# Decode attention with a sliding window: output projection on two column groups, and one more pair of K loads in 32 KB rows

## The chip, the cores and the metric

The kernel runs on one core of a Trainium2 chip. The metric is the device time of one execution in microseconds (us). Each execution also has a span, from its first to its last instruction, some 1.7 us shorter.

## The reference

One query token for each of 32 batch rows, 32 query heads on 8 KV heads, the last 512 positions of a cache of 2048:

```python
q = (x @ wq).reshape(B, Sq, Hq, Dh).transpose(0, 2, 1, 3)      # x 32x512, wq 512x4096
k = repeat(k_cache[:, :, Sk - W:, :], 4); v = repeat(v_cache[:, :, Sk - W:, :], 4)   # W = 512
p = softmax(q @ k.T * Dh ** -0.5)
out = (p @ v).transpose(0, 2, 1, 3).reshape(B, Sq, Hq * Dh) @ wo   # wo 4096x512
```

K and V are 33.5 MB each, wq and wo 4.2 MB each: 75.5 MB to read, very little arithmetic.

## The kernel before

The cache window is cut into 16 K chunks and 16 V chunks of 2 MB (128 rows of 16 KB). K goes through three buffers and V through four. Every load is issued by SyncE (SP), in the order of a list; each other engine has a list of its own. In the lists, `T8.1` is the second of two VectorE transposes of K chunk 8, `S2` the scores of quad 2 on TensorE, `M2` their maximum on VectorE, `E`, `N`, `C` softmax steps on ScalarE, `P2` the turn of the probabilities, `Z1.0` to `Z1.3` the spread of quad 1's probabilities into a masked operand (VectorE and ScalarE share it), `V0` a product P x V.

```python
DMA_ORDER = "K0 B0 K1 V0 K2 K3 K4 K5 V1 K6 K7 K8 V2 K9 K10 K11 V4 K12 K13 K14 V6 K15 V8 ... V15"
V_PAIRED = (2, 4, 6)                      # these V loads carry two chunks, in 32 KB rows
...
# SP: a K load waits until its buffer (of NK = 3) has been transposed
if n >= NK:
    sp.wait_ge(dve_T, 2 * (n - NK + 1))
sp.dma_start(K_sb[:, n % NK]..., cache_rows(k_cache, n)).then_inc(sem_k[n % NK], 16)
...
# TensorE, output projection: four column groups of 128 outputs
for c in range(4):
    pe.matmul(X_ps[32*c:32*(c+1), 2, 0:128], lhsT=o_sel[:, i, hg, :],
              rhs=wo_sb[:, hg, i, c*128:(c+1)*128], ..., tile_position=(0, 32*c))
...
# then two casts on VectorE (c = 0, 1) and two on ScalarE (c = 2, 3), and the output DMA
```

## Time and profile before

| | before |
|---|---|
| time, 3 executions at first | 187.28 us (187.22 to 187.29) |
| time, all 51 executions in this study | 187.22 to 187.77 us |
| loads | 75.5 MB in one queue, 16 DMA engines busy throughout |
| busiest compute engine | VectorE, 71% |

The loads are served by 16 DMA engines, and one packet is one row of a load: the packet records show 128 packets of 16 KB for a load of 2 MB, and 16 in flight at a time. The queue runs dry when fewer are, but for the tens of ns of a handover from packet to packet. A load is "ahead" when its issue comes before the packets in front of it have been worked off. Below, **lead** is the time from the start of a load's issue to its first packet; the prediction subtracts the 0.54 us of the issue itself. (Where the load in front has rows of the same size, as for K13, the first packet is counted off in order of start. On the engine furthest ahead it comes some tenths of a us sooner: in e13 K12's first packet at 100.03 and eight packets of 613 ns give an estimate of 104.9 for K13, the count 105.5.) The profile lines of before, of an execution of 187.45 us, stand in the prediction.

### The profile page before, as it was taken

How to read it: one execution, taken by the hardware profiler on the slowest of the kernel's cores; microseconds unless marked ns; L12 is line 12 of the kernel's file. 1: busy time of each engine (PE TensorE's matmuls, PEld its weight loads, DVE VectorE, ACT ScalarE, POOL GpSimd, SP SyncE). 2: the span in 40 equal slices, each digit the busy share in tenths (PEclk: the TensorE clock that was granted, in tenths of full speed). 3: DMA queues.
4: the chain of work that ended last, by engine and by line, in shares of the span. 5: the costliest groups of instructions: out<-in, count | busy, mean ns of one | idle time of the engine just before them, and what ended most of it. 6: DMA issues, size and time to landing. Idle time of an engine off the chain costs nothing.

```text
span 185.7 us, 3839 instructions
## 1 busy us (share of the span) xinstructions
PE 108.6 (58%) x1604; PEld 88.0 (47%) x1604; DVE 131.4 (71%) x239; ACT 82.6 (44%) x142; POOL 31.2 (17%) x82
## 2 busy tenths in 40 slices
PE   0220303447048983199504996438999995999852
PEld 0100001132038771199203496207987894999741
DVE  0018696999999999939999489999999946510001
ACT  3000100139620069610893033977959899911011
POOL 7100029510600236000330140000021000000000
PEclk9999999999756999759955599655899999699999
DMA  6999999999999999999999999999999999999980
GB/s 201 427 441 420 438 430 416 441 420 438 423 413 441 416 441 445 399 438 420 438 446 402 430 427 427 462 409 406 432 420 434 423 420 434 416 430 407 403 324 24
DMA packets 5872, 75.80 MB, mean 408 GB/s; under 512 B 672, under 2 KB 864, under 8 KB 1888
## 3 DMA queue, kind: packets, MB, share of 16 engines
q1 hardware_dynamic: 5808, 75.53, 96.3%
q8 instruction: 12, 0.20, 0.4%
q10 hardware_dynamic: 48, 0.03, 0.1%
q14 instruction: 4, 0.03, 0.0%
HBM read 75.53 MB, written 0.03 MB: 407 GB/s over the span
## 4 chain that ended last, share of the span: by engine, by line
DMA 45%; PE 22%; DVE 20%; issue 6%; SPq 4%; ACT 0%; DVEq 0%
DMA K_sb<-in_k_cache_dram 26%; PE O_ps L360 14%; DVE KT_sb L436 12%; DMA w_sb<-in_wo_dram 12%; DMA V_sb<-in_v_cache_dram 8%; PE S_ps L321 7%; DVE w_sb L458 6%; SPq L216 2%; DVE maxv L443 2%; PE PT_ps L340 1%; SPq L210 1%; SPq L203 1%; SPq L197 0%; ACT P_bf L506 0%; PE X_ps L397 0%
## 5 line engine op out<-in xcount | busy, mean ns | idle before, releaser
L436 DVE STREAM_TRANSPOSE KT_sb<-K_sb 128x2048 uint32<-128x2048 uint32 x32 | 73.0, 2298 | 13.1 <-DMA K_sb<-in_k_cache_dram 13.0
L360 PE MATMUL O_ps<-w_sb,V_sb 128*128 128x128 bf16 x640 | 42.1, 230 | 3.7 <-DVE w_sb L458 3.1
L360 PEld LDWEIGHTS O_ps<-w_sb,V_sb 128*128 128x128 bf16 x640 | 40.8, 103 | 6.1 <-DVE w_sb L458 3.9
L525 ACT ACTIVATE w_sb<-PTc,mask 128x512 bf16<-128x512 bf16 x60 | 38.5, 730 | 0.0
L270 POOL COPY QBD<-QA_sb 32x64 bf16<-32x64 bf16 x64 | 24.8, 529 | 78.8 <-PE S_ps L321 56.3
L321 PE MATMUL S_ps<-KT_sb,QBD 128*32 128x512 bf16 x256 | 22.3, 504 | 18.1 <-POOL QBD L270 11.0
L458 DVE TENSOR_SCALAR w_sb<-PTc,mask 128x512 bf16<-128x512 bf16 x100 | 30.8, 379 | 0.0
L340 PE MATMUL PT_ps<-P_bf,pick 128*128 128x128 bf16 x128 | 12.6, 277 | 29.8 <-ACT P_bf L506 25.5
L340 PEld LDWEIGHTS PT_ps<-P_bf,pick 128*128 128x128 bf16 x128 | 10.9, 128 | 33.5 <-ACT P_bf L506 28.3
L321 PEld LDWEIGHTS S_ps<-KT_sb,QBD 128*32 128x32 bf16 x256 | 8.3, 115 | 28.7 <-issue 13.8
L497 ACT ACTIVATE X_ps<-S_ps,negmax 128x512 f32<-128x512 f32 x8 | 5.3, 657 | 30.7 <-DVE negmax L445 30.7
L535 ACT ACTIVATE oT_sb<-O_ps 128x128 bf16<-128x128 f32 x8 | 5.9, 741 | 23.9 <-PE O_ps L360 23.9
L525 ACT ACTIVATE K_sb<-PTc,mask 128x512 bf16<-128x512 bf16 x24 | 15.4, 723 | 1.6 <-DVE KT_sb L436 1.6
L360 PE MATMUL O_ps<-K_sb,V_sb 128*128 128x128 bf16 x256 | 15.1, 217 | 1.2 <-DMA V_sb<-in_v_cache_dram 1.2
L360 PEld LDWEIGHTS O_ps<-K_sb,V_sb 128*128 128x128 bf16 x256 | 14.5, 96 | 1.9 <-issue 1.9
L458 DVE TENSOR_SCALAR K_sb<-PTc,mask 128x512 bf16<-128x512 bf16 x40 | 10.7, 347 | 4.4 <-ACT PTc L516 4.4
L360 PE MATMUL O_ps<-KT_sb,V_sb 128*128 128x128 bf16 x128 | 9.1, 240 | 2.5 <-DMA V_sb<-in_v_cache_dram 2.5
L360 PEld LDWEIGHTS O_ps<-KT_sb,V_sb 128*128 128x128 bf16 x128 | 8.9, 108 | 2.6 <-issue 2.6
L301 PE MATMUL X_ps<-w_sb,oT_sb 128*32 128x512 bf16 x32 | 3.8, 626 | 10.6 <-DMA w_sb<-in_wq_dram 10.6
L516 ACT ACTIVATE PTc<-PT_ps 128x512 bf16<-128x512 f32 x8 | 4.8, 594 | 10.5 <-PE PT_ps L340 10.5
L479 DVE CAST K_sb<-S_ps 128x256 bf16<-128x256 f32 x1 | 0.4, 424 | 12.7 <-PE S_ps L372 12.7
L506 ACT ACTIVATE P_bf<-X_ps,recip 128x512 bf16<-128x512 f32 x8 | 5.5, 687 | 8.0 <-DVE recip L451 8.0
(41 smaller groups left out, 49.5 us busy)
## 6 DMA issues: line engine op xcount, KB each, us to landing
K_sb<-in_k_cache_dram SPq DMA_DIRECT2D x16, 2048.0 KB, 17.2
V_sb<-in_v_cache_dram SPq DMA_DIRECT2D x10, 2048.0 KB, 17.0
V_sb<-in_v_cache_dram SPq DMA_DIRECT2D x3, 4096.0 KB, 24.3
w_sb<-in_wq_dram SPq DMA_DIRECT2D x2, 2048.0 KB, 11.8
w_sb<-in_wo_dram SPq DMA_DIRECT2D x7, 512.0 KB, 20.0
w_sb<-in_wo_dram SPq DMA_DIRECT2D x1, 384.0 KB, 21.4
w_sb<-in_wo_dram SPq DMA_DIRECT2D x1, 128.0 KB, 17.5
oT_sb<-in_x_dram ACTq DMA_DIRECT2D x1, 32.0 KB, 4.4
```

The source lines that it names most:

```text
L270: pool.tensor_copy(dst[:, i, :, x0:x0 + 4], src).then_inc(pool_qbd, 1)
L301: ins = pe.matmul(X_ps[32 * c:32 * c + 32, k, :], lhsT=xT_sb[:, kt, :], rhs=w_sb[:, kt, c * 1024 + k * 512:c * 1024 + (k + 1) * 512], star ...
L321: ins = pe.matmul(S_ps[32 * c:32 * c + 32, q % 2, :], lhsT=QBD[:, q % 2, g, b, e, :], rhs=bass.AP(tensor=KT_sb, offset=s0 * slot + (b * G ...
L340: ins = pe.matmul(PT_ps[:, r, :], lhsT=pick[:, r, KS - s:KS - s + P], rhs=P_bf[:, s, :], start=(s == 0), stop=(s == KS - 1), tile_position ...
L360: ins = pe.matmul(O_ps[:, q % 2, 0:P], lhsT=V_sb[:, m % NV, r, :], rhs=z_of(q)[:, :, x0 + r, :], start=(e == 0 and r == 0), stop=(e == 1 a ...
L436: dve.transpose(KT_w[:, n % NK, b].rearrange("p i r s -> p r i s"), K_w[:, n % NK, :, 32 * b:32 * b + 32],).then_inc(dve_T, 1)
L458: ins = dve.tensor_scalar(z_of(q)[:, k].rearrange("p x r -> p (x r)"), PTc[:, q % RING].rearrange("p x r -> p (x r)"), mask[:, k:k + 1], N ...
L497: act.activation(P_f32, S_ps[:, q % 2, :], ACTF.Exp, bias=negmax[:, q:q + 1], scale=SCALE, accum_out=sums[:, q:q + 1],).then_inc(act_exp, 1)
L506: act.activation(P_bf[:, :, :], P_f32.rearrange("p (x s) -> p s x", s=KS), ACTF.Copy, scale=recip[:, q:q + 1],).then_inc(act_P, 1)
L516: act.activation(PTc[:, q % RING], PT_ps[:, :, :].rearrange("p r x -> p x r"), ACTF.Copy).then_inc(act_PT, 1)
L525: ins = act.activation(z_of(q)[:, k].rearrange("p x r -> p (x r)"), PTc[:, q % RING].rearrange("p x r -> p (x r)"), ACTF.Copy, scale=mask[ ...
L535: act.activation(oT_sb[:, :, 4 * q:4 * q + 4].rearrange("p h a -> p a h"), O_ps[:, q % 2, 0:P].rearrange("p (a h) -> p a h", a=4), ACTF.Co ...
```

## The change

The intent is to shave the two ends of a kernel that is bound by its loads: fewer, larger rows in the stream, and a shorter tail of projection and casts after the last load. The order lists were reworked to match the pair.

```diff
-  K0 B0 K1 V0 K2 K3 K4 K5 V1 K6 K7 K8 V2 K9 K10 K11 V4 ...          (DMA_ORDER)
+  K0 B0 K1 K2 V0 K3 K4 K5 K6 V1 K7 K8 V2 K9 K10 V4 ...
-  ... S4 P4 S5 V4 P5 V5 ...                                          (PE_ORDER)
+  ... S4 P4 V4 S5 V5 P5 ...
-  ... T9.0 T9.1 T10.0 Z2.0 T10.1 M4 Z2.1 T11.0 R4 Z2.2 T11.1 Z2.3 M5 R5 T12.0 T12.1 ...   (DVE_ORDER)
+  ... T9.0 T9.1 Z2.0 Z2.1 M4 Z2.2 T10.0 R4 Z2.3 T10.1 T11.0 T11.1 T12.0 M5 T12.1 R5 ...
   (further small moves in DVE_ORDER and ACT_ORDER, and the semaphore counts of the pair, left out)
+  K_PAIRED = (10,)
-  if n >= NK:
-      sp.wait_ge(dve_T, 2 * (n - NK + 1))
+  k = 2 if n in K_PAIRED else 1
+  if n + k > NK:
+      sp.wait_ge(dve_T, 2 * (n - NK + k))
-  K_sb[:, n % NK]..., cache_rows(k_cache, n)
+  K_sb[:, n % NK:n % NK + k]..., cache_rows(k_cache, n, k)
-  for c in range(4):   X_ps[32*c:32*(c+1), 2, 0:128], rhs=wo_sb[:, hg, i, c*128:(c+1)*128]
+  for c in range(2):   X_ps[32*c:32*(c+1), 2, 0:256], rhs=wo_sb[:, hg, i, c*256:(c+1)*256]
-  two casts of 32x128 on VectorE, two on ScalarE
+  one cast of 32x256 on VectorE, one on ScalarE
```

The wait line: for K10 with `k = 2` it is `dve_T >= 18`, both transposes of K8. K10 alone waited for 16, those of K7.

## The prediction

> **What bounds the kernel now.** I read the page first for the shares of the span, then the two DMA rows.
>
> ```profile
> span 185.7 us, 3839 instructions
> PE 108.6 (58%) x1604; PEld 88.0 (47%) x1604; DVE 131.4 (71%) x239; ACT 82.6 (44%) x142; POOL 31.2 (17%) x82
> ...
> DMA  6999999999999999999999999999999999999980
> GB/s 201 427 441 420 438 430 416 441 420 438 423 413 441 416 441 445 399 438 420 438 446 402 430 427 427 462 409 406 432 420 434 423 420 434 416 430 407 403 324 24
> ...
> q1 hardware_dynamic: 5808, 75.53, 96.3%
> q8 instruction: 12, 0.20, 0.4%
> ```
>
> No compute engine is above 71%, but the DMA engines stand at 9 in every slice between the first and the last two, and the load queue q1 alone fills 96.3% of sixteen engines' span. I then went to the packet records in the trace. Between 15 us and 178 us I find no moment at which fewer than 16 packets are in flight, so the queue never runs dry. This is a streaming kernel: a head of 1.8 us before the first packet, a stream, and a tail. Everything inside the stream (transposes, softmax, the spread of P, the PV products) only matters if it starves the queue, that is, if an issue comes later than the end of the packets ahead of it.
>
> The waits of the DMA issuer show that it does wait, but early enough:
>
> ```profile
> SPq L203 <- DVE KT_sb L436: 98.4, 13, 13.0
> SPq L210 <- PE O_ps L360: 38.9, 7, 17.9
> ```
>
> A 98.4 us wait looks like the bound and is not. Setting the issue of each load against its first packet gives the lead: smallest at K chunk 8 (issue done at 59.4, first packet at 61.4, so 2.0 us), 3.0 us at K5, 4.2 us at K7, and 5 to 20 us for the others after the start.
>
> The chain of waits shows the tail:
>
> ```profile
> 161.09 21.45 DMA w_sb<-in_wo_dram
> 182.53 0.04 issue
> 182.58 0.59 PE X_ps L397 x16
> 183.17 0.02 issue
> 183.19 0.28 DVE oT_sb L482
> 183.47 0.31 DVEq L72
> ```
>
> and the timeline the two evacuations behind it:
>
> ```profile
> 183.19 0.57 ACT L552 ACTIVATE oT_sb<-X_ps 32x128 bf16<-32x128 f32 x2 [5.84 <-PE X_ps L397]
> 183.19 0.59 DVE L482 CAST oT_sb<-X_ps 32x128 bf16<-32x128 f32 x2 [4.69 <-PE X_ps L397]
> 183.85 0.35 SPq L222 DMA_DIRECT2D out_dram<-oT_sb  x1
> ```
>
> The last wo packet ends at 182.42, the last four projection matmuls start at 182.90, the last ends at 183.14, the two casts end at 183.78, the output is issued at 183.85 and the span closes at 185.74.
>
> One more reading of the packets is needed, as the stream has 16 ends. Engines that served no instruction fetch finish near 178.93; the last finishes at 182.42. The 12 instruction packets of q8 take 1.02 to 1.10 us each, and the data packet next to one of them is stretched from 0.61 to about 1.1 us, so a fetch sets its engine back by some 1.55 us. They come one per about 256 PE instructions, at 46.4, 65.7, 74.7, ... 180.7 us. Following packets end to start, fetches 1 and 9 fall on one engine, 2 and 10 on another, which fits a turn of eight engines; two fetches (3.1 us) and a start that is up to 0.43 us later than the first engine's give 178.93 + 3.1 + 0.4 = 182.4, the end that is seen. So the span is set by one DMA engine with its share of 75.5 MB plus two fetches.
>
> **What the Trainium skill says.** "DMA: Bandwidth & Descriptors", section "Why small descriptors are slow", gives a fixed overhead per packet; its example is 256 bytes, and it says nothing of 16 or 32 KB rows. The trace agrees that something fixed is left: median 613 ns for a 16 KB packet, 1216 ns for a 32 KB one. The same page's "Specifications" put the HBM limit of a core at about 358 GB/s and the fabric at 435; this trace runs 408 over the whole span and 410 to 440 in most slices, so the second is the one near, and there is little left to win inside the stream. "Runtime: NRT & Kernel Launch", section "Instruction fetch mechanics", says that a sequencer refills its instructions in 16 KiB blocks of 256 through its own DMA queue; the 12 q8 packets of 16,384 bytes agree. It calls the cost mostly hidden; here, with full DMA engines, it isn't. "TensorE: Matmul & The Clock Gate", section "The mechanism" of column tiles, gives the span of a pack as one matmul plus 4 ns for each further tile; the trace shows starts 3 to 4 ns apart in groups of four, 219 to 230 ns each.
>
> **The change part by part.**
>
> 1. K10 and K11 as one load of 32 KB rows. Removed: 256 packets of 16 KB, 16 per engine. Added: 128 of 32 KB, 8 per engine. By the medians each pair of rows saves 2 x 613 - 1216 = 10 ns, so 8 x 10 = 0.08 us per engine. The existing V pairs check this: on an engine without fetches a 2 MB load takes 4.89 us and the three V pairs 9.70 to 9.71, against 9.78, again 0.08. All of it lies in the bound stream, so it counts in full: -0.08 us. The issue that disappears (0.54 us on the issuer) counts nothing, as the issuer was ahead.
>
> 2. Output projection in two groups of 256. Before, the last sub-step is four matmuls 128 wide: 182.898 to 183.137, 0.24 us. After it is two of 256. From the trace at full clock, 128 columns take 219 ns and 512 columns 386 to 388, so 256 take about 219 + 167/3 = 275 ns; with the second start 3 ns later, 0.28. That is +0.04 us. The casts shrink: two of 128 columns in sequence (0.59 us with the gap) become one of 256, and the trace has one such VectorE cast, 128x256 from PSUM, at 0.42 us: -0.17. On ScalarE 272 ns at 128 columns and 491 at 384 give about 0.38 at 256 by the straight line, so VectorE still ends last. Net -0.13 us, fully on the path.
>
> 3. 64 matmuls and 64 weight loads fewer. 3254 recorded PE-side instructions become 3126. At one fetch per 256 that is still 12 (3072). The last fetch may move in time or vanish, but it does not sit on the engine that ends last, so I count 0.
>
> 4. The reordered lists. K2 comes ahead of V0 and K6 ahead of V1, which lets the transposes of K2 start at about 31 instead of 32.8 and moves the leads of K5 to K8 from 3.0, 8.5, 4.2, 2.0 to something better by 0.5 to 2 us. But no lead was negative, so this gains nothing. The cost: the pair must wait for the transposes of K8 (T8.1), as K11 did, where K10 alone waited for T7.1. In the trace T8.1 ends at 77.4 and K9's last packet on the earliest engine at 80.75; an issue is followed by its first packet about 1.0 us later (0.80 to 1.82 at the start), so the lead left is about 80.75 - 78.4 = 2.3 us, where K10 had 11.5. T8.1 should come up to 1 us earlier with the earlier K2, so some 3 us. That is positive: 0.
>
> Sum: -0.08 - 0.13 = -0.21, so 187.28 - 0.21 = 187.07 us. The trace's span would be about 185.5.
>
> **The rivals.**
>
> *The pair starves the queue.* If T8.1 slips by more than about 3 us, all engines idle for the excess and the span grows by it. For it: this is the one lead that falls from double digits. Against: VectorE works almost without a pause from T5.1 to T8.1 (from 58.8 to 77.4 it idles only 0.4 us), so there is no long wait that could grow, and these pieces stand in the same order in the new list. If it happened I expect 0.5 to 2 us, 187.6 to 189.
>
> *Fetches land otherwise.* The end belongs to an engine with two fetches. If the new program shifts the turn so that another engine, with a different start offset, gets the pair, the end moves by up to 0.3 either way; if a third fetch lay on one engine, +1.5; if the engine with fetches 1 and 9 were spared, only down to 182.14, where the next engines end: -0.28. For it: 128 fewer instructions and other times. Against: the assignment looks like a fixed turn, and the three runs of before agree within 0.07 us.
>
> *Later K11, later compute, new bound.* K10 and K11 now land together, so T10 comes about 5 us later and the later softmax steps could push the last PV beyond the last wo landing. Against: selection ends and the projection can start at 178.55, and for 182.9 it has to have done only some 28 groups of four at 56 ns, 1.6 us; that leaves some 2.7 us. The V loads from V10 on have leads of 6 to 9 us. A slip under these is hidden, and the list puts the late pieces in the old order.
>
> *The 256 wide groups are slower.* If two tiles did not overlap, the last sub-step would take some 0.45 us instead of 0.28 and the gain in the tail would vanish: 187.2.
>
> **Range and chances.** All certain terms are tenths of a microsecond, and 2% is 3.7 us. The low end takes the sum and the fetch luck: 187.07 - 0.3 = 186.77. The high end takes no gain in the tail and a small starve or unlucky turn: about 187.4. I give 186.8 to 187.4. Faster by 2% would need the bytes to shrink, which they don't: 0.01. Slower by 2% needs a starve of almost 4 us: 0.02.
>
> **What would show it.** Right: q1 packets fall by 128 + 16 to 5664; 16 engines busy from 15 us to the end; K pair issued near 76 to 78 us and its first packet near 80.8; projection matmuls x64; single casts of about 0.42 and 0.38 us; last wo packet near 182.3; q8 still 12. Wrong: a DMA slice below 9 near 80 us (starved), a last wo packet off by more than 0.3 us with full slices (fetch turn), or an idle PE ahead of the projection that waits for the selection and not for wo.

## More of the kernel before

"Times" below are all executions of a version, not a selection.

## The result

| | times, us | median |
|---|---|---|
| changed, first 6 executions | 186.98, 187.04, 187.63, 187.71, 187.75, 188.22 | 187.67 |
| before, with them | 187.22 to 187.56 | 187.31 |
| changed, all 21 executions | 186.91 to 188.73 | 187.20 |

The ratio of the first six was 1.001, with an interval of 0.9986 to 1.0034: the same within 2%. A ratio here is the mean time of one kernel's runs over that of the other's of the same rounds, so it is not quite the ratio of the medians quoted.

The median of 187.67 lies outside the predicted 186.8 to 187.4. What stands out is the spread. Seven of the 21 executions of the changed kernel are at 187.6 or over and four above 187.8; of 51 executions of the kernel before, five are at 187.6 or over and none above 187.8. The other fourteen of the changed kernel, 186.91 to 187.53, are about where the prediction has them. Luck has a part in the first median: four of the seven slow executions are among the first six, and the fifteen that followed have a median of 187.19. Two questions: did the gains come as reckoned, and where do the slow executions come from?

The profile after was taken of the execution of 186.98 us, a quick one. Its page, with busy tenths in forty slices of the span:

```profile
span 185.3 us, 3707 instructions
PE 109.4 (59%) x1540; PEld 89.4 (48%) x1540; DVE 131.4 (71%) x238; ACT 81.5 (44%) x141; POOL 32.1 (17%) x82
...
DMA  6999999999999999999999999999999999999980
...
q1 hardware_dynamic: 5664, 75.53, 96.5%
q8 instruction: 12, 0.20, 0.4%
```

There are 144 packets fewer in q1, as reckoned, still 12 instruction packets, and full DMA slices. The chain of waits ends so (start, length, what):

```profile
161.39 20.81 DMA w_sb<-in_wo_dram
182.20 0.04 issue
182.25 0.63 PE X_ps L398 x8
...
182.90 0.41 DVE oT_sb L484
```

and the timeline of the casts and the output:

```profile
182.90 0.38 ACT L551 ACTIVATE oT_sb<-X_ps 32x256 bf16<-32x256 f32 x1 [5.88 <-PE X_ps L398]
182.90 0.41 DVE L484 CAST oT_sb<-X_ps 32x256 bf16<-32x256 f32 x1 [4.72 <-PE X_ps L398]
183.37 0.35 SPq L223 DMA_DIRECT2D out_dram<-oT_sb  x1
```

From the end of the last load's wait (182.20) to the end of the casts (182.90 + 0.41 = 183.31) are 1.11 us; before it was 182.53 to 183.78, 1.25 us. The tail gave 0.14 us.

The issuer's waits look almost as before:

```profile
SPq L204 <- DVE KT_sb L439: 100.3, 12, 13.7
SPq L211 <- PE O_ps L361: 38.7, 6, 19.8
```

One wait fewer on each line, a little more on the first. Which wait is the dangerous one can't be seen from a sum.

### The profile page after: what moved, and what is told of

It reads as the page before. It is cut to its first block, busy times and chain, and to the rows that moved or that the text cites. A ratio compares the mean times of both kernels' runs of the same rounds, so it can differ in the third digit from the quotient of the medians.

```text
span 185.3 us, 3707 instructions
## 1 busy us (share of the span) xinstructions
PE 109.4 (59%) x1540; PEld 89.4 (48%) x1540; DVE 131.4 (71%) x238; ACT 81.5 (44%) x141; POOL 32.1 (17%) x82
## 4 chain that ended last, share of the span: by engine, by line
DMA 40%; DVE 22%; PE 20%; issue 7%; ACT 7%; SPq 3%; DVEq 0%
DMA V_sb<-in_v_cache_dram 13%; PE O_ps L361 13%; DMA w_sb<-in_wo_dram 11%; DVE KT_sb L439 10%; DMA w_sb<-in_wq_dram 9%; DMA K_sb<-in_k_cache_dram 6%; DVE w_sb L461 6%; PE S_ps L322 4%; ACT w_sb L525 4%; DVE QA_sb L427 2%; SPq L217 2%; DVE maxv L446 2%; ACT KT_sb L525 1%; PE PT_ps L341 1%; PE X_ps L302 1%
## 5 line engine op out<-in xcount | busy, mean ns | idle before, releaser
L361 PE MATMUL O_ps<-w_sb,V_sb 128*128 128x128 bf16 x640 | 44.7, 238 | 7.9 <-DVE w_sb L461 5.3
L361 PEld LDWEIGHTS O_ps<-w_sb,V_sb 128*128 128x128 bf16 x640 | 43.5, 107 | 9.8 <-DVE w_sb L461 6.1
L271 POOL COPY QBD<-QA_sb 32x64 bf16<-32x64 bf16 x64 | 25.7, 543 | 82.3 <-PE S_ps L322 59.9
L322 PE MATMUL S_ps<-KT_sb,QBD 128*32 128x512 bf16 x256 | 20.6, 473 | 15.4 <-POOL QBD L271 11.0
L322 PEld LDWEIGHTS S_ps<-KT_sb,QBD 128*32 128x32 bf16 x256 | 7.6, 109 | 25.3 <-POOL QBD L271 11.9
L361 PE MATMUL O_ps<-K_sb,V_sb 128*128 128x128 bf16 x256 | 15.1, 217 | 2.2 <-DMA V_sb<-in_v_cache_dram 2.2
L361 PEld LDWEIGHTS O_ps<-K_sb,V_sb 128*128 128x128 bf16 x256 | 14.5, 96 | 3.0 <-issue 3.0
L491 ACT ACTIVATE KT_sb<-X_ps 128x512 bf16<-128x512 f32 x1 | 0.6, 597 | 17.3 <-PE X_ps L302 17.3
L361 PE MATMUL O_ps<-KT_sb,V_sb 128*128 128x128 bf16 x128 | 7.5, 217 | 1.0 <-DMA V_sb<-in_v_cache_dram 1.0
L525 ACT ACTIVATE KT_sb<-PTc,mask 128x512 bf16<-128x512 bf16 x12 | 8.0, 734 | 0.0
```

The lines of the kernel that those rows point to most:

```text
L271: pool.tensor_copy(dst[:, i, :, x0:x0 + 4], src).then_inc(pool_qbd, 1)
L322: ins = pe.matmul(S_ps[32 * c:32 * c + 32, q % 2, :], lhsT=QBD[:, q % 2, g, b, e, :], rhs=bass.AP(tensor=KT_sb, offset=s0 * slot + (b * G ...
L361: ins = pe.matmul(O_ps[:, q % 2, 0:P], lhsT=V_sb[:, m % NV, r, :], rhs=z_of(q)[:, :, x0 + r, :], start=(e == 0 and r == 0), stop=(e == 1 a ...
L525: ins = act.activation(z_of(q)[:, k].rearrange("p x r -> p (x r)"), PTc[:, q % RING].rearrange("p x r -> p (x r)"), ACTF.Copy, scale=mask[ ...
```

## The experiments

I held three theories of the slow executions. **A**: the pair K10/K11 leaves so small a lead that the queue runs dry in some executions. **B**: instruction fetches land on other DMA engines with the new instruction count. **C**: some other part of the new lists is late at times. All versions gave correct results.

### Parts of the change

**e1: the changed kernel again.** No edit.

> The changed kernel once more, to see whether its spread (186.98 to 188.22 in six runs, where the kernel before has 187.22 to 187.56) is its own. Theory A (the paired load leaves the load queue only a small lead, so that it runs dry in some executions), theory B (an instruction fetch lands on another DMA engine in some executions, because of the new instruction count) and theory C (the new lists make a later load or the tail late in some executions) all expect the spread again: single times from 187.0 to 188.2, median near 187.6. If the spread was the chip's, times stay within 0.3 us near 187.1.

Measured: 187.00, 187.13, 187.20, 187.28, 188.01, 188.73, median 187.24 (before in the same rounds 187.34). The spread is the kernel's own. The prediction's time is the quick kind, and the two slow ones are wide apart.

**e2: only the projection**, on the lists and loads of before.

```diff
-for c in range(4):  ... 0:128
+for c in range(2):  ... 0:256        (and the casts)
```

> The kernel before with only the projection in two groups of 256: 64 matmuls and 64 weight loads fewer, lists and loads as before. Expected gain from the tail 0.13 us, so about 187.15 with before at 187.28. Theory A and C: tight, spread under 0.4 us. Theory B: the instruction count is that of the changed kernel, so the spread of over 1 us comes here too, median about 187.6.

Measured: 187.08 to 187.32, median 187.21, ratio 0.9990 (interval 0.9978 to 1.0002). Tight, and 0.13 under the median of before, though the interval does not exclude no gain. Theory B is unlikely: the instruction count is the changed kernel's.

**e3: only pair and lists**, projection as before.

```diff
-for c in range(2):  ... 0:256
+for c in range(4):  ... 0:128        (in the changed kernel)
```

> The changed kernel with the old projection in four groups of 128: pair and lists new, instruction count as before. Theory A and C: the spread is here, single times up to 188.3. Theory B: tight, about 187.2 (only the 0.08 us of the pair gained).

Measured: 187.23, 187.26, 187.38, 187.59, 187.65. No time up to 188.3 came in five, so the expectation of A and C is only half met. But the trace, of the execution of 187.59, was telling: near 81 us 22 packets of 32 KB took 1.3 to 2.4 us where 1.22 is normal, and up to two engines at a time had no packet at all.

**e4: the changed kernel without the pair**, K10 and K11 in their new place as two loads.

```diff
-K_PAIRED = (10,)          ... K9 K10 V4 ...
+K_PAIRED = ()             ... K9 K10 K11 V4 ...
```

> The changed kernel with K10 and K11 as two loads again, in the same place of the new lists. K10 then waits for the transposes of K7 only and has a lead over 10 us. Theory A: tight, about 187.15 (tail gain only). Theory B and C: the spread stays, single times up to 188.2.

Measured: 187.12 to 187.48, median 187.24. Tight enough for A; five executions alone don't rule out C.

### The dose: T8.1 earlier and later

The pair waits for T8.1. Moving that one instruction in the VectorE list moves the lead and little else.

**e5: T8.1 one piece earlier.**

```diff
-T8.0 M3 Z1.1 T8.1 R3 Z1.2 Z1.3 T9.0
+T8.0 M3 T8.1 Z1.1 R3 Z1.2 Z1.3 T9.0
```

> The changed kernel with two neighbours of the VectorE list swapped: the second transpose of K8 (T8.1) ahead of the piece Z1.1 of the spread. The pair K10/K11 waits for T8.1 alone, so its issue comes some 1.3 us earlier and its lead (issue to first packet, 3.4 us in the profiled run of the changed kernel, 2.0 in its repeat, 2.4 with the old projection) rises to 3.3 to 4.8 us. Theory A (the pair is issued too late in some executions and the queue runs dry): spread gone, all times within 187.0 to 187.4, median about 187.1. Theory C (another piece of the new lists) or B (fetches): spread stays, times over 187.9 in a third of the runs.

Measured: 187.06, 187.13, 187.32, 187.35; lead in the trace 4.3 us. None is slow; at one slow in three, four quick ones would come by chance one time in five, so e14 repeats it.

**e6: T8.1 one piece later.**

```diff
-T8.0 M3 Z1.1 T8.1 R3 Z1.2 Z1.3 T9.0
+T8.0 M3 Z1.1 R3 Z1.2 T8.1 Z1.3 T9.0
```

> The opposite: T8.1 behind R3 and Z1.2 instead of ahead, some 1.3 us later. Theory A: the lead falls to 0.7 to 2.1 us, a DMA slice near 81 us is below full, nearly every run is slow, median 188.2 to 188.8. Theories B and C: as the changed kernel, median about 187.3.

Measured: 186.98, 187.03, 187.56, 188.04, 188.23, 188.43, median 187.80. Not nearly every run slow, as A had it: three of six are over 188. The profiled one is the quickest: lead 1.86 us and eight stretched packets (1.3 to 2.0 us) near 81 us, and yet 186.98. A small bubble can be free. My explanation, which no run tests by itself: the end belongs to the engine that is furthest behind, and that one still has packets when the leading engines wait.

**e7: T8.1 two pieces later.**

```diff
-T8.0 M3 Z1.1 T8.1 R3 Z1.2 Z1.3 T9.0
+T8.0 M3 Z1.1 R3 Z1.2 Z1.3 T8.1 T9.0
```

> T8.1 behind Z1.3 as well, some 2.7 us later than in the changed kernel. Theory A: lead about 0.5 us or below, the queue empty for 1 to 2 us, every run slow, median 189 to 190, and about 1.3 us over the run with one piece. Theories B and C: median about 187.3.

Measured: 188.82, 188.94, 189.34, 189.79, median 189.14, ratio 1.0098. Every execution is slow, 1.3 us over e6 in the median, as A said. The page shows the hole; first its DMA row and the GB/s row in forty slices:

```profile
DMA  6999999999999999989999999999999999999980
GB/s 210 424 438 427 424 438 427 420 434 431 420 427 431 417 462 434 389 294 420 432 441 413 424 438 448 431 427 410 429 420 431 424 420 431 431 417 403 408 339 15
```

The eighteenth slice, 80 to 84 us, falls to 294 GB/s. In the packet records of that trace as few as three of the sixteen engines have a packet at 82 us. The timeline of the issuer:

```profile
63.45 17.89 SPq L204 DMA_DIRECT2D K_sb<-in_k_cache_dram  x2
81.39 0.60 SPq L211 DMA_DIRECT2D V_sb<-in_v_cache_dram  x1
```

The first line merges the issues of K9 (at 63.45) and of the pair, which ended at 63.45 + 17.89 = 81.34. The packets of K9 on the first engine had ended by then. The lead of this trace is 1.3 us all the same: the first packet waited for the issue, so about 1.3 us is the least that a lead can be here, however late the issue.

**e8: T8.1 early and T5.1 ahead of Z0.3**, to give K8 a longer lead too.

```diff
-Z0.2 T5.0 Z0.3 T5.1 T6.0 ... T8.0 M3 Z1.1 T8.1 R3
+Z0.2 T5.0 T5.1 Z0.3 T6.0 ... T8.0 M3 T8.1 Z1.1 R3
```

> T8.1 early as above, and T5.1 ahead of Z0.3, which K8 waits for: its lead from 2.7 to some 4 us. If the smaller spread of the kernel before (187.2 to 187.7) comes from the short lead of K8, this one has times within 0.2 us and a median of 187.0; if not, it is like the run with T8.1 early alone.

Measured: 187.15, 187.22, 187.35, 188.00, 188.15, 188.40. A miss: it was to be the tightest. But its profile fell on a slow execution, 188.15, and shows where the scatter starts. The timeline of TensorE, first in the quick execution of the changed kernel, where L361 is V0 and then V1, L322 the scores S2:

```profile
56.52 5.02 PE L361 MATMUL O_ps<-w_sb,V_sb 128*128 128x128 bf16 x64 [4.38 <-DVE w_sb L461]
61.47 2.01 PE L322 MATMUL S_ps<-KT_sb,QBD 128*32 128x512 bf16 x32
63.42 3.78 PE L361 MATMUL O_ps<-w_sb,V_sb 128*128 128x128 bf16 x64
```

in e1 (the same program):

```profile
56.48 6.51 PE L361 MATMUL O_ps<-w_sb,V_sb 128*128 128x128 bf16 x64 [4.34 <-DVE w_sb L461]
62.92 2.00 PE L322 MATMUL S_ps<-KT_sb,QBD 128*32 128x512 bf16 x32
```

and in the slow execution of e8:

```profile
59.05 6.57 PE L361 MATMUL O_ps<-w_sb,V_sb 128*128 128x128 bf16 x64 [6.41 <-DVE w_sb L461]
65.55 2.01 PE L322 MATMUL S_ps<-KT_sb,QBD 128*32 128x512 bf16 x32
```

The same 64 matmuls take 3.78 us at full clock (V1 above), and 5.0 to 6.6 us here, as more or less of V0 falls in a stretch of half clock. The clock records of the traces put that stretch at 49.0 to 59.2 us in the profile after, at 48.7 to 62.3 in e1 and at 47.9 to 65.0 in e8. S2 comes behind V0 and the maximum M2 on VectorE waits for S2. The same line in the timeline of VectorE, first before, then after, then e1, then e8:

```profile
63.66 0.69 DVE L443 TENSOR_REDUCE maxv<-S_ps 128x1 f32<-128x512 f32 x1 [0.37 <-PE S_ps L321]
```

```profile
63.54 0.69 DVE L446 TENSOR_REDUCE maxv<-S_ps 128x1 f32<-128x512 f32 x1 [0.47 <-PE S_ps L322]
```

```profile
64.98 0.69 DVE L446 TENSOR_REDUCE maxv<-S_ps 128x1 f32<-128x512 f32 x1 [1.95 <-PE S_ps L322]
```

```profile
67.60 0.69 DVE L446 TENSOR_REDUCE maxv<-S_ps 128x1 f32<-128x512 f32 x1 [4.20 <-PE S_ps L322]
```

The bracket is the idle time ahead of it. Everything from M2 to T8.1 is packed on VectorE, so this wait is passed on in full to the issue of the pair: from the profile after to e1 it grew by 1.48 us, and the issue came 1.45 us later. The issuer's timeline, after, then e1, then e8:

```profile
63.10 14.74 SPq L204 DMA_DIRECT2D K_sb<-in_k_cache_dram  x2
```

```profile
63.06 16.23 SPq L204 DMA_DIRECT2D K_sb<-in_k_cache_dram  x2
```

```profile
63.43 16.59 SPq L204 DMA_DIRECT2D K_sb<-in_k_cache_dram  x2
```

The pair's issue ends at 77.84, at 79.29 and at 80.02 us, in e8 even with T8.1 a piece earlier. The leads are 3.4, 2.0 and 1.3 us. In e8 the packets near 81 us took up to 2.1 us, and K13 and K14 came short too, near 106 and 111 us (packets of 16 KB up to 2.0 us). Its last wo packet ended at 183.2, against 182.1 in the profile after. So my extra move had hurt: Z0.3 came later, V0 waits for Z0.3 and started at 59.05 instead of 56.5, and the pair lost more than T8.1 had gained. Set from K9's first packet, that of K12 came 0.9 us later here than in the profile after, and that of K15 1.3 us later: about two thirds of the loss is at the pair, the rest at K13 and K14 behind it.

### Taking the clock out of the path

**e9: S2 ahead of V0 on TensorE.**

```diff
-S1 P1 V0 S2 V1 P2
+S1 P1 S2 V0 V1 P2
```

> The changed kernel with one pair of neighbours of the TensorE list swapped: scores S2 ahead of the PV product V0. In the four traces read so far V0 took 5.0 to 6.6 us, depending on how much of it fell in a stretch of half clock (3.8 at full clock), and S2, the maximum M2, T7, T8.1 and the issue of the pair all came later by that difference. With S2 first its length no longer reaches VectorE: the issue of the pair should come at 76.6 to 77.4 us in every execution, a lead of 3.3 us or more. Theory A with the clock as the source: all times within 187.0 to 187.4, median about 187.1. If the source is another: single times over 187.9 in a third of the runs.

Measured: 187.05, 187.31, 187.50, 187.85, 187.97, 188.35. A miss, with a plain reason in its trace: M2 no longer waits, but Z1.0 does, for V1, which has moved back with V0:

```profile
69.83 1.40 DVE L461 TENSOR_SCALAR w_sb<-PTc,mask 128x512 bf16<-128x512 bf16 x5 [1.55 <-PE O_ps L361]
```

The pair was issued at 78.65 instead of the 76.6 to 77.4 that I had expected. The same TensorE work stands ahead of T8.1, through another wait.

**e10: another pair**, K12 with K13, on the lists of before, with the new projection.

```diff
-K_PAIRED = (10,)       (lists of the change)
+K_PAIRED = (12,)       (lists of before:  ... K10 K11 V4 K12 K14 V6 ...)
```

> A version that should keep both gains: projection in two groups, lists of the kernel before, and K12 with K13 as the pair instead of K10 with K11. K13 was issued at 94.4 us in the kernel before and K12 has its first packet at 100.2, so the pair has a lead of some 5.8 us. Theory A: tight, median 187.05 (tail 0.13 and pair 0.08 gained on 187.3), no time over 187.5. If 32 KB rows themselves make the time vary, times over 187.9 appear.

Measured: 187.06, 187.19, 187.29, 187.37, 187.82. Four tight and one not. In its trace the pair had a lead of 6.5 us, but V10 one of 2.7, and from 139.2 to 140.2 us up to three engines at a time had no packet (1.2 us in all, added over the engines), with V10's packets stretched to 1.2 us. So this version has a short lead of its own, at V10; its trace is of a quick execution (187.19), and what made the 187.82 was not caught.

**e11, e12: the changed kernel.** No edit.

> The changed kernel, one look with a trace, in the hope of a slow execution of it (3 of 12 so far were at or over 188.0). Theory A: if this one is over 187.6, its V0 took 6 us or more, the pair was issued after 78.5 us and packets of 32 KB near 81 us took over 1.3 us (1.22 is normal); if it is under 187.3, the issue came before 78.8.

> As the look before: one more chance of a slow execution, with the same tie between the length of V0, the issue of the pair and the time.

Measured: 187.53 and 187.07. In the first V0 took 5.70 us, M2 waited 1.13 us, the pair was issued at 78.22, and packets near 81 us were stretched, on average by 0.19 us per engine. In the second V0 took 5.17 and the issue was at 77.76. This is the expected order, but the first is not a slow execution, and e16 below speaks against it.

### What was still open

**e13: T8.0 and T8.1 ahead of Z1.0, M3 and Z1.1.**

```diff
-T7.1 Z1.0 T8.0 M3 Z1.1 T8.1 R3
+T7.1 T8.0 T8.1 Z1.0 M3 Z1.1 R3
```

> The changed kernel with both transposes of K8 ahead of Z1.0, M3 and Z1.1 in the VectorE list. Z1.0 waits for the PV products V0 and V1, M3 for S3; with S2 first these still held the pair back (Z1.0 idled 1.55 us for V1). Now T8.1 waits only for K8 and M2 and should end near 73.5 to 75 us: lead of the pair 5.5 to 7 us. Late-pair theory: all times in 187.0 to 187.5, none at 187.8 or over. If the scatter has another source, one to three of the runs are over 187.8.

Measured: 187.12, 187.18, 187.23, 187.60, 187.65, 187.95. The lead was 6.8 us in the trace, yet three of six are at 187.6 or over: a miss. There is a second source of scatter, at least here. The pieces of Z1 came later in exchange, and with them the later steps; K13 had a lead of 3.9 us, where before it had 11.3; but e5 had 3.9 there too and was tight.

**e14: e5 once more, and e15: the changed kernel, in the same rounds. e16: the changed kernel.**

> The run with T8.1 ahead of Z1.1 once more, as it had only four times: 187.06 to 187.35. Late-pair theory: again nearly all under 187.5; at most one execution with a very long V0 above.

> The changed kernel in the same rounds on the same chip: late-pair theory: a third of the times at 187.6 or over, as so far (6 of 14).

> One more look for the trace of a slow execution of the changed kernel. If over 187.8: V0 over 6 us, pair issued at 79.3 us or later, packets near 81 us stretched on the engine that ends last too.

Measured: e14 187.06, 187.06, 187.09, 187.13, 187.18, ratio 0.9983 (interval 0.9971 to 0.9995). e15 five times 187.14 to 187.21 and once 187.89, median 187.19, fewer slow ones than the third expected. e16 186.91, the quickest of all. Yet its pair had a lead of 3.0 us and eight packets stretched to 1.3 to 2.4 us, on average by 0.19 us per engine, as much as in e11 at 187.53. With e5, nine executions of the version with T8.1 early lie within 0.3 us.

**e17: e5, and T10.1 earlier**, which K13 waits for. **e18: e13, with the same.**

```diff
-Z2.0 Z2.1 M4 Z2.2 T10.0 R4 Z2.3 T10.1 T11.0
+Z2.0 Z2.1 M4 T10.0 R4 T10.1 Z2.2 Z2.3 T11.0
```

> T8.1 ahead of Z1.1 (nine times so far 187.06 to 187.35) and, besides, both transposes of K10 straight after M4, so that K13, which waits for T10.1, is issued some 3 us earlier: its distance from issue to first packet from 4 to 5 up to 7 or 8 us. Late-load theory (short leads of the pair K10/K11 and of K13 are what the new lists added): the tightest of all, 187.05 to 187.3, median 187.1.

> The version with T8.0 and T8.1 ahead of Z1.0 had a lead of 6.8 us for the pair and still three of six times at 187.6 or over; its K13 had only 3.9 us. Here K13 is brought forward as well. If its short lead made that scatter: all times under 187.5. If three of six stay at 187.6 or over, the scatter there comes from neither load and stays open.

Measured: e17 186.92, 187.00, 187.19, 187.22, 187.35, median 187.19, ratio 0.9983 (interval 0.9971 to 0.9995). e18 187.01, 187.04, 187.14, 187.20, 187.40, 187.69, so one of six at 187.6 or over, where e13 had three, and not all under 187.5. K13's lead was 8.0 us in e17 and 6.4 in e18.

The trace of e17 is the best evidence for the mechanism, as its V0 is as long as that of the slow e8. Its timeline of TensorE and of the issuer:

```profile
56.60 6.58 PE L361 MATMUL O_ps<-w_sb,V_sb 128*128 128x128 bf16 x64 [4.34 <-DVE w_sb L461]
```

```profile
63.17 14.39 SPq L204 DMA_DIRECT2D K_sb<-in_k_cache_dram  x2
```

The pair's issue ends at 77.56, the lead is 3.6 us, no packet near 81 us is stretched, and the execution took 187.19. The clock still moves; with this lead it moved nothing at the end.

**Together.** e5, e14 and e17 have fourteen executions, 186.92 to 187.35 with a median of 187.13, where before has 187.22 to 187.77 and the change 186.91 to 188.73. Against before it is a gain of about 0.2 to 0.3 us, far under 2% (e5 alone does not show it: ratio 0.9994, interval 0.9979 to 1.0008). Against the fourteen quick executions of the change, with a median of 187.16, no gain is shown. What is gone are the slow ones: none of fourteen, against seven of 21, which chance alone would give about one time in sixty.

## Why the prediction was wrong

**Part 1, the pair: right.** Set from K9's first packet (75.86 us before, 75.85 after) the first packet of K12 came at 100.23 and at 100.16, so 0.06 us earlier, for 0.08 reckoned. Other traces bear it out: 24.29 to 24.31 us from K9 to K12 with the pair and no stretched packets (after, e5, e13, e14, e17, e18), 24.32 to 24.38 without the pair (before, e2, e4). The median packet of 32 KB is 1216 ns before and 1215 after. The two profiles differ by more, 187.45 against 186.98 us: the last wo packet came at 182.10 instead of 182.42, and not 0.08 but 0.32 us sooner. That is not the pair's doing alone, as this end lies anywhere from 182.02 to 182.31 in e5, e14 and e17; the rest is chance between executions, as far as the traces tell.

**Part 2, the tail: right.** 0.14 us gained for 0.13 reckoned. The casts took 0.41 and 0.38 us for 0.42 and 0.38. e2, which has this part alone, gained 0.13 in the median, within its noise.

**Part 3, the fetches: right as a zero.** Twelve q8 packets before and after, and e2 with the new instruction count is tight.

**Part 4, the lists: wrong, and this is the step that failed.** In the profiled execution it looks right: the pair issued at 77.30, its first packet at 80.74, both as foreseen. But the prediction took the lead of one trace for the lead of the kernel. Against its first rival, that the pair starves the queue, it said that VectorE "works almost without a pause from T5.1 to T8.1 (from 58.8 to 77.4 it idles only 0.4 us), so there is no long wait that could grow". The 0.37 us ahead of M2 was just such a wait. It is the remainder of TensorE's work over VectorE's: the traces of before, after, e11 and e1 have it at 0.37, 0.47, 1.13 and 1.95 us with V0 at 5.0, 5.0, 5.7 and 6.5 us, under a clock whose stretches begin and end elsewhere in each execution. (In e8 it is 4.20 us, but there V0 also started 2.5 us late.) VectorE, packed, passed the wait on to the issue of the pair. The margin was too large as well: "about 3 us" counted on a T8.1 that would come earlier. With the first packet 1.3 us after the issue's start (e7, e8) and the queue at its end at 80.7 us, T8.1 could end no later than about 79.4, by this estimate, which leaves 2.1 us after 77.3. The page "TensorE: Matmul & The Clock Gate" of the Trainium skill, section "What's actually happening", says that the window in which activity is judged runs freely and isn't reset by a kernel, and that the same kernel meets a different number of slow matmuls in each run. The half clock stretches of these traces agree, with 10.2, 13.7 and 17.1 us for the same one in after, e1 and e8. The prediction used the page for its column tiles alone.

The expected extra microsecond from the earlier K2 did not come either. T8.1 ended at about 77.3, as before, since VectorE falls in step with TensorE again at V0, which started at 56.5 instead of 56.6 us.

**The rivals.** The first was the right one, with the right cost (0.5 to 2 us), and was given too little weight. The dose of e5, e6 and e7, with e14 and e17, shows that a late issue of the pair costs time; e4 without the pair and the bubbles seen in e3, e7 and e8 fit it. The late compute rival and the fetch rival, as far as the instruction count goes, showed nothing: e2 is tight, and in the quick trace TensorE started the projection at 178.24 and then waited for wo. The fourth, wide groups slower, fell with part 2.

**The range.** It rested on three executions that agreed within 0.07 us. In 51 the kernel before spans 0.55. The high end of 187.4 held 13 of the 21 executions of the changed kernel, but not the median of the first six. The median of all 21, 187.20, lies in the range, and 0.19 us under the 187.39 of the 51 before, for 0.21 reckoned: the sum was right for the quick executions, and what it left out is the slow third.

**What stays open.** No execution of the changed kernel over 187.6 us was caught with a trace; its slow executions are put down to the pair by the dose and by its siblings, not by a trace of their own. The mean granted clock does not sort them either: 186.98 ran at 0.853 and 188.22 at 0.872. Between leads of 1.9 and 3.4 us the traces show no clean order: e6 with 1.86, e1 with 1.96, e9 with 1.97 and e16 with 2.98 were quick, e3 with 2.39 and e11 with 2.46 were slower, and e16, the quickest of all, had as much stretching as e11. Only under 1.4 us (e7, e8) is it plain. Nor is all the loss at the pair: in e3 and e11 K12's first packet came 0.3 and 0.1 us later than in the profile after, and K15's 0.6 and 0.3. The kernel before scatters by 0.55 us without the pair, and no run here tells why; the engines that the fetches fall on were not followed from execution to execution. And e10, e13 and e18 still have single executions at 187.6 to 188.0 that the pair's lead does not explain. K13's short lead is a weak candidate: bringing K13 forward took e13's three slow of six to one of six, which is too few to show it, and e5 was tight with the same short lead, as was e4 with 4.3 us. For e10 the short lead of V10 is one.

## What to carry to other kernels

In a kernel bound by its loads, list for each load the time from issue to first packet, and treat the shortest as a risk, not as a margin: find what the issue waits for, back through every engine, and ask how much that varies from one execution to the next. Joining two loads saves a little (here 10 ns for each two rows of 16 KB), but makes both wait for what the second waited for; choose the pair by its lead, or move what it waits for forward in the list. Judge such a change by many executions, since one profile of a quick execution shows only the gains.

## What the Trainium skill lacked or had wrong

- "DMA: Bandwidth & Descriptors" has no figure for how far ahead of the end of the queue a load must be issued. Here a lead of 3.4 us or more, from the start of the issue to the first packet, left all 32 KB packets of the pair at their length (after, e5, e13, e14, e17, e18), 1.9 to 3.1 us some of them stretched, in six traces without a clear cost (e1, e6, e9, e12, e15, e16), and 1.3 us left engines empty or packets stretched to about 2 us (e7, e8).
- The same page says nothing of rows above the small ones in its section on slow descriptors: 16 KB packets took 613 ns and 32 KB packets 1216 ns, so 10 ns are left to gain for each pair of such rows.
- "Runtime: NRT & Kernel Launch" calls the cost of an instruction fetch mostly hidden. With full DMA engines each of the 12 fetches held one engine for 0.95 to 1.10 us (traces before and after), and the engines ended up to 3.5 us apart (178.9 to 182.4 us in the kernel before).
- "TensorE: Matmul & The Clock Gate" reckons the ramp at under 1% of a typical span. No page tells that its shift from run to run can reach the loads through the waits: here the same 64 matmuls took 5.0 to 6.6 us and moved the issue of a load by 1.45 us in the same program (77.30 and 78.75 us).
